# Second layer of a small MLP by seven block products in place of eight, at the end of a fused attention and MLP kernel

## The chip, the core and the metric

The kernel runs on one core of one Trainium2 chip. The metric is device microseconds of one execution: before the change the median of 3 runs is 971.51 us (971.46 to 971.6). The engines are named as in the profile: PE (TensorE matmul), PEld (its weight loads), DVE (VectorE), ACT (ScalarE), POOL (GpSimd), SP (the queue that issues nearly all DMAs).

## What is computed

Attention over 4 batches, 12 heads, 448 positions and 64 dimensions; its output is read as 1792 tokens of 768 numbers and goes through two MLPs. The change is in the last line:

```python
x = attn_out.transpose(0, 2, 1, 3).reshape(1792, 768)
h = x @ w_in;  x = (h * sigmoid(h)) @ w_out             # first MLP, 768 -> 2048 -> 768
h = x @ w_in2                                           # second MLP, 768 -> 1024
e = exp(h - max(h));  solu = h * e / sum(e)
ln = (solu - mean) / sqrt(var + 1e-6) * g_ln
out = ln @ w_out2                                       # second layer, 1024 -> 768
```

## The kernel before

All matrix products of the MLPs run in float32r with each operand split in two: a rounded half "hi" and the rest "lo". Each product is then three matmuls (list HL: hi by lo, lo by hi, hi by hi) summed in a PSUM bank.

**First MLP.** Its hidden size is cut into 8 groups g, its tokens into 4 blocks b of 512, 512, 512 and 256. A step (g, b) has two parts on PE: mlp1_a (L808, 36 matmuls) makes the hidden values, ACT applies Silu twice (L814, L815) and POOL makes the lo half (L816); mlp1_b (L831, 36 matmuls) multiplies by w_out, and DVE adds the result into x2 (L837). The list flow puts mlp1_a of a step ahead of mlp1_b of the step before.

**Weights.** They arrive as float64 bit patterns. A piece is 128x384. For each, stages() gives a chain of operations: load (L127, SP), magnitude (L135, ACT), clamp, shift, sign, low (L138 to L150, DVE), hi (L159, or L161 and L163 where the gain g_ln is folded in, ACT), lo (L171, POOL) and, for weights that are needed later, two stores to DRAM (L174). enqueue() gives every operation a due time in a clock that counts PE work (a piece every EV[0] = 3.55), and tick() issues what is due between the matmuls. During group g, ahead() queues the 8 pieces of the weights of group g+1 (fetch) and then 8 pieces of two of the ten "parked" slabs: the last group's weights, the four slabs of w_in2 and the four of w_out2. w_out2 is prepared during groups 4 and 5. A slab is 128 x 2 x 1536 (hi and lo). unpark (L725) loads it back with two DMAs of 768 KB, into the pool big as its buffers come free.

**Second MLP.** It works on 14 tiles t of 128 tokens. split (L853 POOL, L854 DVE) makes hi and lo of a tile of x2. moe2_a(t) (L922) is the first layer, 36 matmuls of 512 columns. moe2_n(t) is the softmax gate and the layer norm: peak, power, over, gate, stats, rstd, norm (L934 to L960). moe2_t (L971 to L974) turns the result with 8 transposes, and makes its halves from PSUM (hi on ACT, lo on DVE). moe2_b(t) (L995) is the second layer: two column ranges of 384, each 24 matmuls into one bank, then a copy (L1002) and a store (L1006; L1004 for the last tile, which is cut 512 and 256). In the steady state PE runs moe2_a(t), moe2_b(t-2), transposes of t-1, moe2_a(t+1) and so on.

The schedule is written out by hand (tc.manual_schedule()): each engine runs its instructions in the order in which the Python code issues them.

Of the kernel before, what the change touches and what calls it, by code (L numbers as in the profile page):

```python
# [24 lines left out]
SLAB = 1536  # L25
# [72 lines left out]
def fused_kernel(ctx: ExitStack, tc, nat, qt, gqk, w_in, w_out, w2_in, w2_out, g_ln, out):  # L98
# [9 lines left out]
    sm_ = ctx.enter_context(tc.tile_pool(name="sm", bufs=2))  # L108

    nc.scalar.preload_act_table_set("natural_log_exp_and_others")  # L110
    CL, LO = "vvvv", 'pppp'

    def stages(w, src, g, ph, c, park=None):
# [8 lines left out]
        s = slice(c * n, (c + 1) * n)  # L122
# [30 lines left out]
        def hi():  # L153
            if park is None:
                k["hi"], k["lo"] = w()[:, 0, s], w()[:, 1, s]
            else:
                k["hi"], k["lo"] = k["a"].bitcast(F32R), k["t"].bitcast(F32R)
            if g is None:
                nc.scalar.copy(out=k["hi"], in_=k["tf"])  # L159
            else:  # L160
                nc.scalar.activation(out=k["hi"], in_=k["tf"], func=AF.Identity, scale=g[:, c // 2:c // 2 + 1])  # L161
                if LO[ph] == "p":
                    nc.scalar.activation(out=k["tf"], in_=k["tf"], func=AF.Identity, scale=g[:, c // 2:c // 2 + 1])  # L163

        def lo():
            tf, h = k["tf"], k["hi"].bitcast(F32)
            if g is not None and LO[ph] == "v":
                nc.vector.scalar_tensor_tensor(out=k["lo"], in0=tf, scalar=g[:, c // 2:c // 2 + 1], in1=h,
                                               op0=ALU.mult, op1=ALU.subtract)
            else:  # L170
                en[LO[ph]].tensor_tensor(out=k["lo"], in0=tf, in1=h, op=ALU.subtract)  # L171

        def store(i):
            nc.sync.dma_start(out=park[:, i, s], in_=(k["af"], k["tf"])[i])  # L174
        return [load, mag, clamp, shift, sign, low, hi, lo] + \
            ([lambda: store(0), lambda: store(1)] if park is not None else [])

# [519 lines left out]
    STEP = ((0, 3.0, 4.2, 4.8, 5.4, 6.0, 7.2, 8.4), (0, 4.5, 5.7, 6.3, 6.9, 7.5, 8.7, 9.9, 9.9, 11.5))  # L697
# [6 lines left out]
    def enqueue(pool, keep, src, every, g=None, ph=1, at=None, park=None):  # L704
        i = len(keep)
        if park is None:
            keep.append(None)

        def w():
            if keep[i] is None:  # L710
                keep[i] = slab(pool)
            return keep[i]
        for c in range(SLAB // 384):
            if at is not None:
                last[0] = at + every * c
            else:
                last[0] = max(last[0] + every, clock[0])
            for x, f in zip(STEP[ph > 0], stages(w, src, g, ph, c, park)):
                due.append((last[0] + x, len(due), f))
        due.sort(key=lambda x: x[0])  # L720

    def unpark(pool, keep, park):
        t = slab(pool)
        for i in range(2):
            nc.sync.dma_start(out=t[:, i, :].bitcast(F32), in_=park[:, i, :])  # L725
        keep.append(t)
# [33 lines left out]
    acc1 = ctx.enter_context(tc.tile_pool(name="acc1", bufs=1, side="right", reuse_waits="tile"))  # L760
    psx = ExitStack()
    ps_mm = ctx.enter_context(tc.tile_pool(name="ps_mm", bufs=2, space=PSUM, side="right", reuse_waits="tile"))
    gp = ctx.enter_context(tc.tile_pool(name="gp", bufs=2, side="right", reuse_waits="tile"))
    cvx = ctx.enter_context(ExitStack())
    P_["cv"] = cvx.enter_context(tc.tile_pool(name="cv3", bufs=3, side="right", reuse_waits="tile"))
    x2 = [acc1.tile([128, KD, CW[0]], F32, name="x2_0")]
    big2x, psy = ExitStack(), ExitStack()

    def after_attention():
# [53 lines left out]
    def mlp1_b(i, g, b, gt):  # L823
# [15 lines left out]
        for d in range(KD):  # L839
            L.append((6 * MM[b], lambda d=d: part(d)))  # L840
        return L
# [14 lines left out]
    SPL = (0, 4, 6)  # L856
# [5 lines left out]
    for i, (g, b) in enumerate(steps):  # L862
        gt = []
        if b == 0 and 0 < g < NMG - 2:
            def ahead(g=g):
                fetch(g + 1, EV[0])
                for x in range(2 * g - 2, 2 * g):
                    enqueue(None, [], parked[x][0], EV[0], parked[x][1], ph=2 if x < 6 else 3, park=parks[x])
# [3 lines left out]
        if i == len(steps) - 1:  # L872
            def swap():
                cvx.close()
                P2["x"] = ctx.enter_context(tc.tile_pool(name="xs", bufs=3, side="right", reuse_waits="tile"))
                split(0)
            flow.append((0, swap))
        flow += mlp1_a(g, b, gt)
        if g == NMG - 1:
            def fetch2(b=b):  # L880
                for x in range(2 * b + 2, 2 * b + 4):
                    unpark(big, w2, parks[x])
# [226 lines left out]
```

## Time and profile before

| | |
|---|---|
| median of 3 runs | 971.51 us |
| the profiled execution, its own time | 971.44 us |
| its span, first to last instruction | 969.5 us |
| PE busy | 960.9 us (99%) |
| DVE, ACT, POOL busy | 69%, 46%, 43% |
| granted TensorE clock | 1.000 |
| second MLP on PE | from 718.2 us to about 966.3 us |

The table of busy shares is an average over stages with different limits; the rows of the section on the trace are taken from the stages that the change touches. An operation with a small idle time ahead of it on PE says that PE waited for nothing there.

### The profile page before, as it was taken

Reading aid. Unit: us, or ns where it says so; the run is one execution under the profiler, and the core shown is the slowest. Engines: PE = TensorE matmul, PEld = TensorE weight load, DVE = VectorE, ACT = ScalarE, POOL = GpSimd, SP = SyncE. Lnnn points to the kernel's source line nnn. Section 1 sums busy time; section 2 is a strip of 40 time slices with the busy share of each in tenths; the row PEclk is TensorE's granted clock in tenths of the full one; section 3 lists DMA queues with packets and bytes.
Section 4 is the critical chain, followed back from the end, with each engine's and each line's share of the span. In section 5 each row is a group of like instructions: output and inputs, shape, how many; then the busy total and the mean of one; then the engine's idle time right before and its main releaser. Section 6 shows DMA issues by size and latency. Waiting matters only on the chain.

```text
span 969.5 us, 15059 instructions
## 1 busy us (share of the span) xinstructions
PE 960.9 (99%) x5128; PEld 798.6 (82%) x5128; DVE 672.7 (69%) x1335; ACT 442.1 (46%) x1072; POOL 412.4 (43%) x577
## 2 busy tenths in 40 slices
PE   8999999999999999999999999999999999999998
PEld 8766667767778888888888888888888989999898
DVE  7899999999645789798888888842236535435441
ACT  6998999999722333433433453521102212212121
POOL 7888889888433434444444434431110100101000
PEclk9999999999999999999999999999999999999999
DMA  6776858775312236546364464853330000000001
GB/s 201 201 208 169 226 165 221 198 206 142 113 37 65 79 96 193 156 128 198 102 199 140 141 201 123 278 187 130 135 126 1 24 27 17 33 17 17 33 17 49
DMA packets 56717, 121.16 MB, mean 125 GB/s; under 512 B 9984, under 2 KB 32384, under 8 KB 56640
## 3 DMA queue, kind: packets, MB, share of 16 engines
q1 hardware_dynamic: 56352, 120.19, 41.3%
q8 instruction: 41, 0.67, 0.3%
q14 instruction: 36, 0.29, 0.1%
q10 hardware_dynamic: 288, 0.01, 0.0%
HBM read 77.08 MB, written 21.23 MB: 101 GB/s over the span
## 4 chain that ended last, share of the span: by engine, by line
PE 87%; DVE 5%; ACT 3%; DMA 2%; issue 1%; POOL 1%; SPq 0%; DVEq 0%; POOLq 0%; ACTq 0%
PE hp L808 24%; PE xps L831 24%; PE op L995 12%; PE h L922 12%; PE sp L445 4%; PE pv L540 4%; PE tp L497 3%; DVE sp L453 2%; ACT p L464 1%; PE lp L971 1%; PE pv L543 1%; DVE ms L281 1%; ACT ht L526 1%; DMA nat<-nat 1%; ACT qk L276 1%
## 5 line engine op out<-in xcount | busy, mean ns | idle before, releaser
L808 PE MATMUL hp<-xt,slab 128*128 128x512 f32 (+1 forms) x1152 | 238.1, 364 | 0.0
L831 PE MATMUL xps<-gt,slab 128*128 128x512 f32 (+1 forms) x1152 | 235.8, 363 | 0.0
L808 PEld LDWEIGHTS hp<-xt,slab 128*128 128x128 f32 x1152 | 197.0, 189 | 34.3 <-issue 0.7
L831 PEld LDWEIGHTS xps<-gt,slab 128*128 128x128 f32 x1152 | 197.3, 189 | 33.9
L837 DVE TENSOR_TENSOR x<-xps,x 128x512 f32<-128x512 f32 (+1 forms) x168 | 103.3, 619 | 87.1 <-PE xps L831 86.6
L816 POOL TENSOR_TENSOR gt<-gf,gt 128x512 fp32r<-128x512 f32 (+1 forms) x64 | 78.0, 1218 | 143.3 <-ACT gt L815 127.7
L995 PE MATMUL op<-slab,lt 128*128 128x384 f32 (+2 forms) x672 | 119.3, 335 | 0.0
L922 PE MATMUL h<-slab,xh 128*128 128x512 f32 x504 | 118.1, 392 | 0.0
L995 PEld LDWEIGHTS op<-slab,lt 128*128 128x128 f32 x672 | 116.2, 188 | 1.9
L453 DVE TENSOR_SCALAR_CACHE_REDUCE sp<-sp,ms 128x448 f32<-128x448 f32 x168 | 109.2, 684 | 8.1 <-PE sp L445 5.5
L922 PEld LDWEIGHTS h<-slab,xh 128*128 128x128 f32 x504 | 93.6, 188 | 19.1
L489 POOL TENSOR_SCALAR p<-p,st 128x448 f32<-128x448 f32 x144 | 97.7, 689 | 18.2 <-DVE st L480 10.4
L464 ACT ACTIVATE p<-sp,st 128x448 f32<-128x448 f32 x144 | 96.6, 687 | 6.6 <-DVE sp L453 6.2
L955 POOL TENSOR_SCALAR sm<-sm 128x1 f32<-128x1 f32 x14 | 2.7, 191 | 209.5 <-DVE sm L954 201.7
L814 ACT ACTIVATE gf<-hp 128x512 f32<-128x512 f32 (+1 forms) x64 | 34.8, 543 | 120.9 <-PE hp L808 120.2
L171 POOL TENSOR_TENSOR slab<-cvt,slab 128x384 fp32r<-128x384 f32 x48 | 51.6, 1075 | 82.9 <-ACT slab L159 82.9
L497 PE MATMUL tp<-ident,p 128*128 128x128 f32 x504 | 77.4, 274 | 1.2 <-ACT ht L526 0.9
L159 ACT CAST slab<-cvt 128x384 fp32r<-128x384 f32 x48 | 24.7, 514 | 106.4 <-DVE cvt L150 106.4
L497 PEld LDWEIGHTS tp<-ident,p 128*128 128x128 f32 x504 | 60.8, 140 | 11.2 <-ACT ht L526 2.7
L938 ACT ACTIVATE e<-h,sm 128x512 f32<-128x512 f32 x26 | 17.6, 683 | 109.7 <-DVE sm L935 109.7
L146 DVE SCALAR_TENSOR_TENSOR cvt<-raw,cva 128x384 uint32<-128x384 uint32 x88 | 63.6, 723 | 4.7 <-DVE cva L142 0.4
L171 POOL TENSOR_TENSOR cvt<-cvt,cva 128x384 fp32r<-128x384 f32 x40 | 44.0, 1102 | 52.9 <-issue 29.7
(119 smaller groups left out, 1434.0 us busy)
## 6 DMA issues: line engine op xcount, KB each, us to landing
Z<-X SPq DMA_DIRECT2D x92, 224.0 KB, 3.7
raw<-w_in SPq DMA_DIRECT2D x48, 384.0 KB, 3.4
raw<-w_out SPq DMA_DIRECT2D x48, 384.0 KB, 3.2
slab<-park SPq DMA_DIRECT2D x20, 768.0 KB, 6.2
nat<-nat SPq DMA_DIRECT2D x23, 480.0 KB, 4.0
park<-cva SPq DMA_DIRECT2D x40, 192.0 KB, 1.9
park<-cvt SPq DMA_DIRECT2D x40, 192.0 KB, 2.9
vn<-nat SPq DMA_DIRECT2D x24, 256.0 KB, 3.9
```

What stands on the lines that cost most here:

```text
L146: nc.vector.scalar_tensor_tensor(out=k["t"], in0=k["hw"], scalar=0xC0000000, in1=k["a"], op0=ALU.bitwise_and, op1=ALU.bitwise_or)
L171: en[LO[ph]].tensor_tensor(out=k["lo"], in0=tf, in1=h, op=ALU.subtract)
L453: nc.vector.tensor_scalar(out=sp, in0=sp, scalar1=c["ms"][:, g:g + 1], scalar2=None, op0=ALU.mult, op1=ALU.min, accum_out=c["st"][:, 0, i: ...
L464: nc.scalar.activation(out=P(i), in_=c["sp"][i][:, :], func=AF.Exp, bias=c["st"][:, 0, i:i + 1], scale=-1.0, accum_out=c["st"][:, 1, i:i + 1])
L489: nc.gpsimd.tensor_scalar(out=p, in0=p, scalar1=r, scalar2=0.0, op0=ALU.mult, op1=ALU.add)
L497: nc.tensor.transpose(tp[:, o + t * 128:o + (t + 1) * 128], p[:, a:a + 128], ident[:, :])
L808: nc.tensor.matmul(hp[0][:, 0:CW[b]], ws[g][0][:, pw, kd * 256 + m * 128:kd * 256 + (m + 1) * 128], xT[(b, kd)][:, px, :], start=(i == 0), ...
L816: nc.gpsimd.tensor_tensor(out=gt[0][:, 1, m, :], in0=gf[:, :], in1=gt[0][:, 0, m, :].bitcast(F32), op=ALU.subtract)
L831: nc.tensor.matmul(xps[:, 0:CW[b]], ws[g][1][:, pw, m * 768 + d * 128:m * 768 + (d + 1) * 128], gt[0][:, px, m, :], start=(j == 0), stop=( ...
L837: nc.vector.tensor_tensor(out=x2[b][:, d, :], in0=xps[:, 0:CW[b]], in1=x2[b][:, d, :], op=ALU.add)
L922: nc.tensor.matmul(h2[:, half, :], xh[:, px, kd, :], wt[:, pw, (kd % 3) * 512:(kd % 3 + 1) * 512], start=(i == 0), stop=(i == 3 * KD - 1))
L995: nc.tensor.matmul(op[:, 0:c1 - c0], lt[:, px, k, :], wt[:, pw, o + c0:o + c1], start=(i == 0), stop=(i == 23))
```

## The change

A pair of token tiles is taken as a 2x2 block matrix: A11 and A12 are the two 512-wide halves of the even tile (after the transposes), A21 and A22 those of the odd one. w_out2 with its gain is the 2x2 matrix of 512x384 blocks W11 to W22. The product is made by Strassen's scheme in Winograd's form: S1 = A21+A22, S2 = S1-A11, S3 = A11-A21, S4 = A12-S2, T1 = W12-W11, T2 = W22-T1, T3 = W22-W12, T4 = W21-T2, and seven block products A11 W11, A12 W21, S2 T2, S1 T1, S3 T3, S4 W22, A22 T4 instead of eight.

- **Weights.** enqueue4 takes the four blocks of one 384-wide column piece together: after the gain (ACT, now one operation), DVE makes T1, T3, T2 and T4; seven results are split into halves (hi on ACT, lo on POOL) in a tile "stg" of three buffers and stored with one DMA of 384 KB each. There are seven slabs of w_out2 in DRAM instead of four. The other parked weights use the same stg tile.
- **Tokens.** x2 is also stored to DRAM (x2d) and from tile 4 on loaded back by pairs (stage), so that its room is free for the second MLP; the last three of the seven slabs are loaded there.
- **Second layer.** Per pair: four copies of the transposed halves to SBUF (take), four mixes (S1, S2 on POOL; S3, S4 on DVE), seven splits (cast: ACT, DVE), seven products of 12 matmuls of 384 columns, three copies of partial sums out of PSUM (snap, ACT), three additions (add, DVE), one plain copy (ACT).
- The last pair uses another order of the products (ENDING), and what was after each product is put in by the table hooks.

```diff
+    def enqueue4(src, every, park, c, g):
+        q = {}
+        for x in ("11", "12", "22", "21"):
+            i = 2 * int(x[0]) + int(x[1]) - 3
+            push(stages(src[i], c, 2, {y: p[:, :, s] for y, p in park.items()}, None if g is None else g(x, c), (x, q)),
+                 every)
...
+        def sub(o, a, b):
+            def f():
...
+                nc.vector.tensor_tensor(out=q[o], in0=q[a], in1=q[b], op=ALU.subtract)
+            return f
+        if name == "11":
+            base += out("11", 9.3)
+        elif name == "12":
+            base += [(9.5, sub("T1", "12", "11"))] + out("T1", 10.3)
+        elif name == "22":
+            base += [(9.5, sub("T3", "22", "12"))] + out("22", 9.3) + out("T3", 10.5) + \
+                [(11.1, sub("T2", "22", "T1"))] + out("T2", 11.9)
+        else:
+            base += out("21", 9.3) + [(11.2, sub("T4", "21", "T2"))] + out("T4", 12.0)
...
+    def stage(p):
+        xs[p, "f"] = P2["f"].tile([128, KD, 256], F32, name="xf", tag="xf")
+        nc.sync.dma_start(out=xs[p, "f"][:, :, :], in_=x2d[p // 2][:, :, p % 2 * 256:p % 2 * 256 + 256])
...
+    STEPS = (("11", "11", 0), ("12", "21", 2), ("S2", "T2", 0), ("S1", "T1", 1), ("S3", "T3", 0), ("S4", "22", 1),
+             ("22", "T4", 0))
+    ENDING = (("11", "11", 0), ("12", "21", 2), ("22", "T4", 3), ("S2", "T2", 0), ("S1", "T1", 1), ("S3", "T3", 0),
+              ("S4", "22", 1))
...
+    def cast(x, f):
+        s_ = parts[x] = P2["s"].tile([128, 2, 512], F32R, name="S", tag="S")
+        nc.scalar.copy(out=s_[:, 0, :], in_=f[:, :])
+        nc.vector.tensor_tensor(out=s_[:, 1, :], in0=f[:, :], in1=s_[:, 0, :].bitcast(F32), op=ALU.subtract)
...
-        for c0, c1 in cuts:
-            op = ps_mm.tile([128, 512], F32, name="op", tag="mm")
-            i = 0
-            for k in range(8):
-                wt = w2[4 + k // 2]
-                for px, pw in HL:
-                    o = (k % 2) * 768
-                    nc.tensor.matmul(op[:, 0:c1 - c0], lt[:, px, k, :], wt[:, pw, o + c0:o + c1],
-                                     start=(i == 0), stop=(i == 23))
+        for i, (a, w, b) in enumerate(ENDING if last else STEPS):
...
+            for k in range(4):
                 for px, pw in HL:
+                    nc.tensor.matmul(op[b][:, 0:384], parts[a][:, px, k * 128:(k + 1) * 128],
+                                     W[w][:, pw, k * 384:(k + 1) * 384], start=(n[b] == 1 and j == 0),
+                                     stop=(j == 11), skip_group_check=True)
...
+            if a == "11":
+                snap("P1", 0)
...
+                cast("S4", raws["S4"])
+            elif a == "12":
+                add(0, 0, 2, "P1")
...
+            elif a == "S2":
+                snap("U2", 0)
+            elif a == "S1":
+                snap("P5", 1)
+            elif a == "S3":
+                add(1, 384, 0, "P5")
...
+            elif a == "S4":
+                add(0, 384, 1, "U2")
...
+    for p in range(1, NPR + 1):
+        a, b = 2 * p, 2 * p + 1
+        if p < NPR:
+            if p > 1:
+                turned(a - 2)
+            hs[a] = moe2_a(a)
+            early()
+            turned(b - 2)
+            n = norm(a)
+            do(n[0:3])
+            later(nc.gpsimd, n[3:8])
+            rest()
+            do(n[8:])
+            if p + 1 < NPR:
+                split(a + 2)
+            hs[b] = moe2_a(b)
+            n = norm(b)
+            if p + 1 < NPR:
+                hooks = {0: [lambda: split(b + 2)], 2: n[0:1], 3: n[1:3], 4: n[3:]}
...
+            else:
+                hooks = {0: n[0:3], 1: n[3:4], 2: n[4:6], 3: n[6:8], 4: n[8:] + [lambda: turned(a), early],
+                         6: [lambda: turned(b), lambda: cast("22", raws["22"]), lambda: later(nc.vector)]}
+            moe2_b(p - 1, hooks)
```

PE, second layer, before: one tile in the steady state (op is the PSUM tile of a column range, slab the weights, lt the halves of the turned tile).

```order
L995 MATMUL op_8545<-slab_7676,lt_8483 128x384 x6
L995 MATMUL op_8545<-slab_7679,lt_8483 128x384 x6
L995 MATMUL op_8545<-slab_7879,lt_8483 128x384 x6
L995 MATMUL op_8545<-slab_7882,lt_8483 128x384 x6
L995 MATMUL op_8581<-slab_7676,lt_8483 128x384 x6
L995 MATMUL op_8581<-slab_7679,lt_8483 128x384 x6
L995 MATMUL op_8581<-slab_7879,lt_8483 128x384 x6
L995 MATMUL op_8581<-slab_7882,lt_8483 128x384 x6
```

PE, the same place after the change: one pair of tiles (S is one of the seven split blocks).

```order
L1104 MATMUL op_8902<-slab_7753,S_8807 128x384 x12
L1104 MATMUL op_8925<-slab_7756,S_8810 128x384 x12
L1104 MATMUL op_8902<-slab_7955,S_8843 128x384 x12
L1104 MATMUL op_8958<-slab_7958,S_8846 128x384 x12
L1104 MATMUL op_8902<-slab_8205,S_8850 128x384 x12
L1104 MATMUL op_8958<-slab_8208,S_8917 128x384 x12
L1104 MATMUL op_8902<-slab_8211,S_8939 128x384 x12
```

A tile had 48 matmuls, a pair 96; a pair now has 84, in seven runs of 12, and the bank op_8902 is filled, copied out and added to four times.

DVE, preparation of w_out2 during group 4, after the change (cva and cvt are the working tiles of a piece, xps the PSUM tile of the first MLP; L157 to L169 are the former L138 to L150, L889 the former L837, L189 is new).

```order
L157 TENSOR_SCALAR cva_6546<-cva_6546 128x384
L189 TENSOR_TENSOR cvt_6471<-cvt_6507,cvt_6471 128x384
L889 TENSOR_TENSOR x2_3_3922<-xps_6571,x2_3_3922 128x256
L161 TENSOR_SCALAR cva_6546<-cva_6546 128x384
L889 TENSOR_TENSOR x2_3_3922<-xps_6581,x2_3_3922 128x256
L165 SCALAR_TENSOR_TENSOR cvt_6547<-raw_6492,cva_6546 128x384
L169 SCALAR_TENSOR_TENSOR cvt_6547<-raw_6492,cvt_6547 128x384
L189 TENSOR_TENSOR cvt_6518<-cvt_6507,cvt_6518 128x384
```

Before, the same stretch held L138, L142, L146, L150 and L837 alone; the subtractions L189 (four for each four pieces) stand between them, behind the gain on ACT that they read.

DVE, one pair in the steady state, after the change (S splits, raw and mixed are the blocks in SBUF, h2 the first layer's result of the odd tile).

```order
L1050 TENSOR_TENSOR S_9383<-mixed_9375,S_9383 128x512
L1050 TENSOR_TENSOR S_9386<-mixed_9373,S_9386 128x512
L1058 TENSOR_TENSOR raw_9358<-raw_9301,raw_9358 128x512
L1050 TENSOR_TENSOR S_9390<-raw_9358,S_9390 128x512
L1058 TENSOR_TENSOR raw_9308<-raw_9308,mixed_9375 128x512
L1014 BN_AGGR sm_9368<-sm_9368 128x2
L1020 TENSOR_SCALAR e_9367<-e_9367,sm_9368 128x1024
L916 TENSOR_TENSOR xh_9398<-xf_9193,xh_9398 128x768
L1050 TENSOR_TENSOR S_9457<-raw_9308,S_9457 128x512
L916 TENSOR_TENSOR xh_9460<-xf_9193,xh_9460 128x768
L1089 TENSOR_TENSOR ob_9440<-op_9463,sn_9455 128x384
L1050 TENSOR_TENSOR S_9477<-raw_9365,S_9477 128x512
```

The splits of S2, S1, S3, S4 and A22 stand around the end of the even tile's norm; before, this place held the norm and two splits for each tile.

## Rows read from the trace of the kernel before

**Rows 1.** The page, parts 1 and 2: busy us and shares; tenths in 40 slices.
```profile
PE 960.9 (99%) x5128; PEld 798.6 (82%) x5128; DVE 672.7 (69%) x1335; ACT 442.1 (46%) x1072; POOL 412.4 (43%) x577
PE   8999999999999999999999999999999999999998
```

**Rows 2.** Waits of PE, whole program: who, for whom, us, times, longest.
```profile
PE tp L245 <- POOL ident masks.py:199: 1.3, 1, 1.3
```

**Rows 3.** Timeline of PE over one tile: start, us, operation, count.
```profile
852.45 8.51 PE L995 MATMUL op<-slab,lt 128*128 128x384 f32 x48
860.79 1.03 PE L971 MATMUL lp<-ident,e 128*128 128x128 f32 x8
861.59 8.45 PE L922 MATMUL h<-slab,xh 128*128 128x512 f32 x36
869.87 8.51 PE L995 MATMUL op<-slab,lt 128*128 128x384 f32 x48
```

**Rows 4.** Groups by form, 780 to 930 us: busy us, mean ns | idle before.
```profile
L947 DVE SCALAR_TENSOR_TENSOR e<-h,sm,e 128x512 f32<-128x512 f32 x18 | 12.7, 746 | 0.3
L938 ACT ACTIVATE e<-h,sm 128x512 f32<-128x512 f32 x18 | 12.2, 683 | 81.5 <-DVE sm L935 81.5
L951 DVE BATCH_NORM_STATS2 sm<-e 128x6 f32<-128x512 f32 x18 | 11.5, 680 | 0.0
L934 DVE TENSOR_REDUCE sm<-h 128x2 f32<-128x1024 f32 x9 | 11.0, 1225 | 52.4 <-PE h L922 52.4
L974 DVE TENSOR_TENSOR lt<-lp,lt 128x512 fp32r<-128x512 f32 x16 | 10.3, 686 | 6.5 <-ACT lt L973 6.5
L973 ACT CAST lt<-lp 128x512 fp32r<-128x512 f32 x16 | 8.6, 589 | 0.1
```

**Rows 5.** First preparation of w_out2, 545 to 578 us: busy by engine, then groups.
```profile
545.00:578.00 33.00, 33.00 (x164) 28.03 (x164) 27.04 (x49) 17.51 (x33) 14.72 (x13) 1.00 0.59 186
L171 POOL TENSOR_TENSOR cvt<-cvt,cva 128x384 fp32r<-128x384 f32 x8 | 9.3, 1160 | 13.5 <-ACT cvt L163 7.2 <-issue 6.4
L150 DVE SCALAR_TENSOR_TENSOR cvt<-raw,cvt 128x384 uint32<-128x384 uint32 x9 | 7.5, 839 | 0.3
L816 POOL TENSOR_TENSOR gt<-gf,gt 128x512 fp32r<-128x512 f32 x4 | 5.2, 1296 | 4.7 <-ACT gt L815 3.4 <-DMA raw<-w_out 1.3
L837 DVE TENSOR_TENSOR x<-xps,x 128x256 f32<-128x256 f32 x6 | 2.5, 420 | 0.6 <-PE xps L831 0.5
```

**Rows 6.** Timeline of POOL: first and last of 8 pieces, then two slab pieces.
```profile
549.13 1.34 POOL L171 TENSOR_TENSOR cvt<-cvt,cva 128x384 fp32r<-128x384 f32 x1 [3.17 <-ACT cvt L163]
...
577.33 1.29 POOL L171 TENSOR_TENSOR cvt<-cvt,cva 128x384 fp32r<-128x384 f32 x1 [3.31 <-issue]
...
591.74 1.02 POOL L171 TENSOR_TENSOR slab<-cvt,slab 128x384 fp32r<-128x384 f32 x1 [2.50 <-ACT slab L159]
...
605.96 1.01 POOL L171 TENSOR_TENSOR slab<-cvt,slab 128x384 fp32r<-128x384 f32 x1 [2.36 <-ACT slab L159]
```

**Rows 7.** Timeline of PE and DVE around the start of group 6.
```profile
602.93 8.32 PE L808 MATMUL hp<-xt,slab 128*128 128x512 f32 x36
...
604.18 0.56 DVE L146 SCALAR_TENSOR_TENSOR cvt<-raw,cva 128x384 uint32<-128x384 uint32 x1
...
606.09 1.30 DVE L146 SCALAR_TENSOR_TENSOR cvt<-raw,cva 128x384 uint32<-128x384 uint32 x1
```

**Rows 8.** The stretch of four slab loads: busy by engine, clock, DMA, GB/s.
```profile
690.00:695.00 5.00, 5.00 (x24) 4.14 (x23) 2.57 (x4) 0.21 (x1) 1.29 (x1) 1.00 1.02 423
```

**Rows 9.** The end, and DMA issues (count, KB each, us to landing).
```profile
966.55 0.37 ACT L1002 COPY ob<-op 128x256 f32<-128x256 f32 x1 [2.24 <-PE op L995]
...
raw<-w_out SPq DMA_DIRECT2D x48, 384.0 KB, 3.2
park<-cva SPq DMA_DIRECT2D x40, 192.0 KB, 1.9
y<-ob SPq DMA_DIRECT2D x1, 128.0 KB, 1.7
```

More of the change, by code (lines that the diff above doesn't have):

```diff
@@ L165, in lo @@
[L165 to L174, printed above, removed]
@@ L175, in stages, with gain @@
-        return [load, mag, clamp, shift, sign, low, hi, lo] + \
-            ([lambda: store(0), lambda: store(1)] if park is not None else [])
+        base = list(zip(STEP[ph], (load, mag, clamp, shift, sign, low)))
+        if quad is None:
+            return base + list(zip(STEP[ph][6:], halves(lambda: k["tf"], w, CL[ph])))
+        name, q = quad
+        def gain():
+            if g is not None:
+                nc.scalar.activation(out=k["tf"], in_=k["tf"], func=AF.Identity, scale=g)
+            q[name] = k["tf"]
@@ L702, in tick, with push, enqueue @@
             due.pop(0)[2]()
-    def enqueue(pool, keep, src, every, g=None, ph=1, at=None, park=None):
+    def push(fs, every, at=None):
+        last[0] = at if at is not None else max(last[0] + every, clock[0])
+        for x, f in fs:
+            due.append((last[0] + x, len(due), f))
+        due.sort(key=lambda x: x[0])
+    def enqueue(pool, keep, src, every, ph=1, at=None, park=None):
         i = len(keep)
@@ L872, in fused_kernel @@
         if i == len(steps) - 1:
[L873 to L877, printed above, removed]
+            flow += [(0, lambda: split(0)), (0, lambda: split(1))]
         flow += mlp1_a(g, b, gt)
@@ L1028, in fused_kernel @@
         tick(dur)
[L1029 to L1032 removed]
+    assert not due
     psx.close()
     P2["l"] = ctx.enter_context(tc.tile_pool(name="ps_l", bufs=2, space=PSUM, side="right", reuse_waits="tile"))
[L1035 to L1059 removed]
@@ new lines, in fused_kernel @@
+    split(2)
+    hs[1] = moe2_a(1)
+    n = norm(1, ())
+    do(n[0:1])
+    split(3)
+    tp = [turn(0, half) for half in range(2)]
+    mlp1.close()
+    P2["e"] = ctx.enter_context(tc.tile_pool(name="me", bufs=3, reuse_waits="tile"))
+    P2["1"] = ctx.enter_context(tc.tile_pool(name="m1", bufs=6, reuse_waits="tile"))
+    P2["s"] = ctx.enter_context(tc.tile_pool(name="ms", bufs=5, reuse_waits="tile"))
+    P2["w"] = ctx.enter_context(tc.tile_pool(name="mw", bufs=3, reuse_waits="tile"))
+    P2["f"] = ctx.enter_context(tc.tile_pool(name="mf", bufs=1, reuse_waits="tile"))
@@ new lines, in fused_kernel @@
+    P2["x"] = ctx.enter_context(tc.tile_pool(name="mx", bufs=2, reuse_waits="tile"))
+    P2["2"] = ctx.enter_context(tc.tile_pool(name="m2", bufs=2, reuse_waits="tile"))
+    P2["3"] = ctx.enter_context(tc.tile_pool(name="m3", bufs=4, reuse_waits="tile"))
+    lns[1] = P2["e"].tile([128, 2, 512], F32, name="e", tag="e")
+    do(n[1:3])
+    for x in USED[4:]:
+        W[x] = unpark(P2["w"], None, park2[x])
+    stage(2)
+    for half in range(2):
+        take(0, half, tp[half])
+    do(n[3:])
```

285 lines of the change are left out of this document (165 added, 120 removed).

## The prediction, made before the changed kernel ran

> **What bounds the kernel now.** I read the page first: PE is busy 99% of the span, and every slice from the second on shows nine tenths or more [rows 1]. A busy PE need not be a working one, so the list of who waited for whom came next: the longest wait of PE in the whole program is 1.3 us, at the very start [rows 2]. So the time is the sum of PE's instructions, and a change is worth what it takes out of that sum, as long as nothing else becomes late. Then the timeline of PE in the second MLP [rows 3]: over one tile the starts of the operations follow one another without a hole. From start to start moe2_b takes 860.79 - 852.45 = 8.34 us (48 matmuls of 384 columns, 0.1738 us each), the 8 transposes 861.59 - 860.79 = 0.80, moe2_a 869.87 - 861.59 = 8.28. The printed durations are some tenths longer, because ends are modelled; I take start to start. The groups by form [rows 4] show DVE and ACT with long idle times ahead of the operations that wait for PE (52.4 us ahead of 9 peaks): they follow PE here. In the stage where w_out2 is prepared it is different: DVE is busy 27.04 of 33 us, POOL 14.72 [rows 5].
>
> **The matmuls.** 14 tiles of 48 are 672; 7 pairs of 7 x 12 are 588. The other matmuls and the transposes stay. 84 x 0.1738 = 14.60 us go, all of it from the chain that sets the end. Form, width and weight loads of the 588 are those of before, so their price is a row of the same thing. Each run of 12 starts behind two waits, but waits that are already met have no visible price: moe2_a and moe2_b follow one another without a hole [rows 3].
>
> **What comes in beside PE, steady state.** A pair has 32.8 us on PE (2 x 8.28 + 1.6 + 84 x 0.1738). DVE gets per pair three more splits (0.69 each), two mixes and three additions of 384 columns (below 0.69 each): some 5 us on top of 16; ACT some 5 on top of 7; POOL two sums of 128x512, 1.30 each by the nearest row of that size [rows 4, 5]. No engine is near 32.8. What can hurt is latency, since all queues are in order. I count from the end of moe2_a of the even tile, t = 0. Transposes until 0.8, two copies on ACT (0.59) until 2.0, S1 and S2 on POOL until 4.6, S2's hi until 5.2. On DVE peak, then (after ACT's two powers, 0.68 each) over, two gates of 0.75 and two stats of 0.68 stand ahead of S2's lo: about 6.9, so lo is there at 7.6. PE wants S2 after 0.8 + 8.28 (moe2_a of the odd tile) + 2 products of 2.085 = 13.25. That is 5.6 us of cover. S3 is ready near 10.5 and wanted at 17.4; S4 stands behind norm and a split, ready near 15, wanted at 19.5. The copies of partial sums have a product of 2.085 us between the end of one fill of a bank and the start of the next, against 0.6 for the copy. So these edits cost nothing; if the cover were gone, each us of lateness would cost 6 us, once per pair before the last.
>
> **Where the cover is thin.** With the last odd tile, peak and both powers move ahead of the copy U2 in ACT's queue, because its norm is spread over the products. My count has that copy end 0.2 us after PE wants the bank. In the last pair all splits follow one another with no moe2_a beside them; S3 there misses its time by about 0.2. The transposes of tile 1, whose norm has only one moe2_a beside it, by 0.1. Together 0.5; nothing in the trace shows these places, so I bound them with 0 and 2 us, and take 0.5 because the count is made of rows of the same operations.
>
> **The end.** Before, a copy of 256 columns (0.37) and a store of 128 KB (1.7) follow the last matmul; then it is an addition of 384 columns on DVE, between 0.42 for 256 [rows 5] and 0.69 for 512 [rows 4], say 0.55, and a store of 192 KB, 1.9 as for a store of that size to DRAM [rows 9]: +0.4 (0 to 0.8).
>
> **The weights, earlier.** Per four pieces there are four subtractions on DVE and seven outputs instead of four. In the 33 us of the first preparation that is 8 x 0.56 (an unhindered DVE operation of the same size [rows 7]) = 4.5 us more on DVE, and 6 x 1.16 = 7.0 more on POOL [rows 5]. DVE then has 31.5 of 33 at least. DVE and POOL hinder one another: with POOL in a slab operation from 605.96 to 606.97, DVE's next one takes 1.30 us, and 0.56 without [rows 6, 7]. With subtractions at the hindered mean of 0.84 and all new POOL time on top, DVE would need 27.0 + 6.7 + 7.0 = 40.7: 7.7 us late at the end of the stage. Who needs it? The next slab is w_in of group 6: its last piece is done at 591.74 + 1.02 = 592.8, and PE starts on it at 602.93 [rows 6, 7]: 10.2 us of cover. A hidden-layer bank of the first MLP is filled in half a section (4.1 us) and wanted again two sections (16.3) after its start: 12.2 us for ACT. So 0 to 7.7 us late costs PE nothing. The second preparation (groups 5 and 6) feeds slabs that are loaded long after.
>
> The outputs go through three buffers. Eight pieces take (577.33 - 549.13) / 7 = 4.03 us each [rows 6], so seven outputs have 16.1 us, 2.3 each, and a buffer may be held 6.9 us. I count hi 0.6, lo 1.2, store 3.2 (a load of 384 KB; two stores of 192 KB would be 3.8) [rows 4, 5, 9]: 5.0 to 5.6, and queueing. It fits, not by much.
>
> **Loads at the turn.** Three slabs and the first token pair, 5.5 MB, are loaded only when the first MLP's room is free. Four loads together moved 423 GB/s [rows 8], so 13 us. Between the end of the first MLP on PE and the fifth product of the first pair lie three moe2_a, two sets of transposes and four products: 34.8 us. The stores of x2 and SP's order stand ahead of it, but twice the time would still fit.
>
> **Sum.** 971.44 (the profiled execution: span 969.5 and 1.94 around it) - 14.60 + 0.5 + 0.4 = 957.7. The median of the runs is 0.07 above that execution, so 957.8.
>
> **Rivals.**
> - *Late weights.* To the 7.7 us of lateness come waits of DVE for the gain on ACT that each subtraction reads, up to 0.6 each by the nearest ACT row [rows 4], 8 x 0.6 = 5. Then w_in of group 6 is 12.7 - 10.2 = 2.5 us late: 960.3. For it: DVE's share and the hindrance. Against: not every wait comes on top. [...] Chance 0.13.
> - *Seven starts are not free.* If every run of 12 begins with a hole of 0.1 us, 49 x 0.1 = 4.9: 962.7. Against: no hole at any border of rows 3. It takes in the case that splits come late by about 0.8 us beyond their cover in each pair. Chance 0.06.
> - *Slower: the three output buffers hold up ACT.* ACT waits for a free stg buffer, and behind it in its queue stand Silu and the magnitudes of the next pieces. If a buffer is held h us, a preparation of 14 outputs is late by 14 x (h/3 - 2.3). At h = 12 that is 23.8 us; the first costs 23.8 - 10.2 = 13.6, the second (cover 12.2, ACT's) 11.6: 983. It turns slower from h of about 10.8, where the two cost 14. For it: SP is one queue in order, and a store that waits for POOL keeps the next load behind it. Against: my count of h is half of that. Chance 0.04.
> - *Nothing gained.* The seven products could go at a lower rate than the eight, for instance by weight loads: 971. But the form is the same. Chance 0.02.
>
> **How the numbers follow.** Forecast 0.75, with its own range of 956.8 (all small terms 0) to 959.5 (2.0 and 0.8, rounded). 8 in 10 needs a part of the late weights too: 956.7 to 961.0. A change of 0.2% (1.9 us) is about what a measurement of this kernel tells from none: faster 0.93, the same 0.02 (nothing gained), slower 0.05 (the buffers, and mechanisms that I don't see).
>
> **What would show it.** Right: PE with 588 matmuls of 384 columns in the second layer at 0.174 us from start to start; a pair of 32.8 us; no wait of PE above 0.5 us after the first MLP; two preparations with DVE above 90%. Wrong: waits of PE on DVE or ACT ahead of a product in each pair (then the latency count fails), a hole ahead of mlp1_a of group 6 or of a Silu bank (then the preparation), or on a slab load at the fifth product (then the turn).

## The result, and the profile after

The changed kernel takes **958.91 us** (median of 4 runs, 958.33 to 959.2) against 971.56 us of the kernel before in the same session (971.46 to 971.84): ratio 0.9869, 95% interval 0.9852 to 0.9886. The forecast was 957.8 with a range of 956.7 to 961.0. So it is 1.1 us slower than forecast, and the range holds it.

The profiled execution took 958.81 us, its span is 957.0. In the kernel after, some lines have other numbers: mlp1_a is L860, mlp1_b L883, Silu L866 and L867, its lo half L868, moe2_a L982, the transposes L1035, the block products L1104, the copies of partial sums (snap) L1086, the additions L1089; in the preparation shift to low are L161 to L169, the gain L179, the subtractions L189, hi L124, lo L127, the store of stg L130 and the load of a slab L768.

The page of the kernel after, part 1 (busy us, share of the span), against [rows 1]:

```profile
PE 946.0 (99%) x5044; PEld 784.5 (82%) x5044; DVE 715.1 (75%) x1410; ACT 471.6 (49%) x1133; POOL 443.5 (46%) x601
```

PE has 84 matmuls less and 14.9 us less of busy time; DVE, ACT and POOL have 42, 30 and 31 us more and are still far from the span. The timeline of PE over one pair of tiles, against [rows 3]:

```profile
774.18 8.44 PE L982 MATMUL h<-slab,xh 128*128 128x512 f32 x36
...
791.51 14.75 PE L1104 MATMUL op<-slab,S 128*128 128x384 f32 x84
806.10 1.04 PE L1035 MATMUL lp<-ident,e 128*128 128x128 f32 x8
806.89 8.44 PE L982 MATMUL h<-slab,xh 128*128 128x512 f32 x36
```

From start to start a pair takes 806.89 - 774.18 = 32.71 us (32.8 were counted), and seven products 806.10 - 791.51 = 14.59, which is 0.1737 per matmul. Two tiles took 2 x 17.42 = 34.84 us before [rows 3], so a pair gives 2.13 us. No row of PE in this stretch has an idle time, and no row of the last two pairs has one either:

```profile
922.33 10.59 PE L1104 MATMUL op<-slab,S 128*128 128x384 f32 x60
...
933.55 4.44 PE L1104 MATMUL op<-slab,S 128*128 128x384 f32 x24
...
938.62 14.81 PE L1104 MATMUL op<-slab,S 128*128 128x384 f32 x84
```

The list of PE's waits (who, for whom, us, times, longest) has one of 1.0 us behind the attention that the kernel before lacks:

```profile
PE hp L860 <- ACT gt L867: 1.0, 1, 1.0
```

The timeline of PE shows its place:

```profile
640.49 8.32 PE L883 MATMUL xps<-gt,slab 128*128 128x512 f32 x36
649.77 8.45 PE L860 MATMUL hp<-xt,slab 128*128 128x512 f32 x36 [0.96 <-ACT gt L867]
658.07 2.20 PE L883 MATMUL xps<-gt,slab 128*128 128x512 f32 x9
```

The same place in the kernel before (mlp1_b is L831 there, mlp1_a L808) has no wait:

```profile
639.91 8.32 PE L831 MATMUL xps<-gt,slab 128*128 128x512 f32 x36
648.07 8.32 PE L808 MATMUL hp<-xt,slab 128*128 128x512 f32 x36
```

After the change, mlp1_b should be followed at 640.49 + 8.16 = 648.65; mlp1_a starts at 649.77 and takes 8.30 us to the next start where its neighbours take 8.16. That is 1.26 us in all. It falls at the end of the second preparation of w_out2.

**Where the span's 12.5 us came from**, from the starts on PE in both traces: the second MLP, from the second moe2_a to PE's end, takes 220.72 us where it took 235.63: -14.91. The wait above: +1.26. The first MLP starts at 254.82 where it started at 254.23: +0.58. From PE's end to the end of the span it is 3.78 where it was 3.21: +0.57. PE's end is its last start plus the prices from start to start, because the printed ends are modelled. The sum is -12.50. The rows, two of before and then three of after, the last of them the final addition on DVE, which stands where [rows 9] have a copy at 966.55:

```profile
254.23 4.34 PE L808 MATMUL hp<-xt,slab 128*128 128x512 f32 x18
730.66 8.35 PE L922 MATMUL h<-slab,xh 128*128 128x512 f32 x36
254.82 4.34 PE L860 MATMUL hp<-xt,slab 128*128 128x512 f32 x18
732.50 8.35 PE L982 MATMUL h<-slab,xh 128*128 128x512 f32 x36
953.47 0.56 DVE L1089 TENSOR_TENSOR ob<-op,sn 128x384 f32<-128x384 f32 x1 [1.00 <-PE op L1104]
```

The chain of work that ended last, just ahead of PE's late start (start, us, what):

```profile
644.40 1.03 POOL stg L127
...
645.46 0.57 DVE cvt L165
...
646.61 0.48 DVE cvt L189
...
647.16 0.07 ACT stg L124
...
647.58 0.62 ACT cvt L179
...
648.64 0.59 ACT gf L866
649.24 0.49 ACT gt L867
```

This is the preparation of the last weight piece, going from POOL to DVE and on to ACT, with a Silu behind it in ACT's queue. DVE had waited 1.89 us for POOL ahead of 645.46: by the code L165 writes a working tile (cvt, three buffers) that POOL's lo half had still to read. In the link that ended last the wait is thus for a working tile, not for an output buffer. Silu reads a PSUM bank that PE had filled some 12 us earlier, at half of the section that ends at 640.49, and PE waits for that bank.

### The profile page after: what moved, and what is told of

Read it like the earlier page. It is cut to its first block, busy times and chain, and to the rows that moved or that the text cites. A ratio compares the mean times of both kernels' runs of the same rounds, so it can differ in the third digit from the quotient of the medians.

```text
span 957.0 us, 15017 instructions
## 1 busy us (share of the span) xinstructions
PE 946.0 (99%) x5044; PEld 784.5 (82%) x5044; DVE 715.1 (75%) x1410; ACT 471.6 (49%) x1133; POOL 443.5 (46%) x601
## 5 line engine op out<-in xcount | busy, mean ns | idle before, releaser
L860 PE MATMUL hp<-xt,slab 128*128 128x512 f32 (+1 forms) x1152 | 238.2, 364 | 1.0 <-ACT gt L867 1.0
L883 PE MATMUL xps<-gt,slab 128*128 128x512 f32 (+1 forms) x1152 | 235.7, 363 | 0.0
L860 PEld LDWEIGHTS hp<-xt,slab 128*128 128x128 f32 x1152 | 197.0, 189 | 35.5 <-ACT gt L867 1.4
L883 PEld LDWEIGHTS xps<-gt,slab 128*128 128x128 f32 x1152 | 197.3, 189 | 33.8
L889 DVE TENSOR_TENSOR x<-xps,x 128x512 f32<-128x512 f32 (+1 forms) x168 | 102.4, 618 | 68.6 <-PE xps L883 68.3
L868 POOL TENSOR_TENSOR gt<-gf,gt 128x512 fp32r<-128x512 f32 (+1 forms) x64 | 78.7, 1230 | 126.4 <-ACT gt L867 111.7
L982 PE MATMUL h<-slab,xh 128*128 128x512 f32 x504 | 117.8, 392 | 0.0
L982 PEld LDWEIGHTS h<-slab,xh 128*128 128x128 f32 x504 | 93.6, 188 | 18.8
L1104 PE MATMUL op<-slab,S 128*128 128x384 f32 x588 | 103.6, 335 | 0.0
L1104 PEld LDWEIGHTS op<-slab,S 128*128 128x128 f32 x588 | 102.2, 188 | 0.5
L127 POOL TENSOR_TENSOR slab<-cvt,slab 128x384 fp32r<-128x384 f32 x48 | 51.8, 1079 | 82.7 <-ACT slab L124 82.7
L866 ACT ACTIVATE gf<-hp 128x512 f32<-128x512 f32 (+1 forms) x64 | 34.7, 542 | 106.5 <-PE hp L860 105.4
L127 POOL TENSOR_TENSOR stg<-cvt,stg 128x384 fp32r<-128x384 f32 x52 | 56.8, 1100 | 56.8 <-ACT stg L124 55.7
L124 ACT CAST slab<-cvt 128x384 fp32r<-128x384 f32 x48 | 24.6, 514 | 107.6 <-DVE cvt L169 107.6
L165 DVE SCALAR_TENSOR_TENSOR cvt<-raw,cva 128x384 uint32<-128x384 uint32 x88 | 63.6, 723 | 10.4 <-POOL stg L127 4.9
L473 PE MATMUL sp<-Z 128*128 128x448 f32 x138 | 64.2, 466 | 2.2 <-ACT X L417 1.1
L473 PE MATMUL sp<-X,lz 128*128 128x448 f32 x168 | 63.3, 379 | 0.5 <-POOL lz L413 0.5
```

Source lines behind the costliest of these rows:

```text
L127: en[e].tensor_tensor(out=k["o"][1], in0=f(), in1=k["o"][0].bitcast(F32), op=ALU.subtract)
L473: nc.tensor.matmul(sp[:, :], a_, k_, start=(w == 0), stop=(w == len(mm) - 1))
L860: nc.tensor.matmul(hp[0][:, 0:CW[b]], ws[g][0][:, pw, kd * 256 + m * 128:kd * 256 + (m + 1) * 128], xT[(b, kd)][:, px, :], start=(i == 0), ...
L868: nc.gpsimd.tensor_tensor(out=gt[0][:, 1, m, :], in0=gf[:, :], in1=gt[0][:, 0, m, :].bitcast(F32), op=ALU.subtract)
L883: nc.tensor.matmul(xps[:, 0:CW[b]], ws[g][1][:, pw, m * 768 + d * 128:m * 768 + (d + 1) * 128], gt[0][:, px, m, :], start=(j == 0), stop=( ...
L889: nc.vector.tensor_tensor(out=x2[b][:, d, :], in0=xps[:, 0:CW[b]], in1=x2[b][:, d, :], op=ALU.add)
```

## Experiments

Two questions: is the price of a product what it was taken for, and where do the covers end; and what makes the second preparation late. The line numbers below are those of the kernel after (one more behind L1058 where S1 is repeated).

### What a product costs: one product twice

```diff
-    STEPS = (..., ("S4", "22", 1), ("22", "T4", 0))
+    STEPS = (..., ("S4", "22", 1), ("22", "T4", 0), ("22", "T4", 0))
```

and ("S4", "22", 1) twice in ENDING; what follows a product in the code stands behind the second of the two.

> The last product of each pair is done twice (12 more matmuls of 384 columns per pair, 84 in all; the sums it goes into are therefore not the reference's). Theory 'PE is the bound and a product costs its matmuls': 958.9 + 84 x 0.1738 = 973.5. Theory 'part of the gain of 14.6 us was given back to waits in the second MLP that an extra product would cover': less than 973.5, by the size of these waits. Theory 'each run of 12 has a price of its own': more than 973.5, 0.7 us for every 0.1 us of price.

Measured: 975.88 us (975.42 to 977.12), 17.0 more than the change. The timeline of PE over a pair, and at the last two pairs:

```profile
776.25 8.44 PE L982 MATMUL h<-slab,xh 128*128 128x512 f32 x36
...
811.03 8.44 PE L982 MATMUL h<-slab,xh 128*128 128x512 f32 x36
...
950.62 0.44 PE L1104 MATMUL op<-slab,S 128*128 128x384 f32 x1 [1.38 <-ACT S L1049]
```

A pair takes 34.78 us, 2.07 more than 32.71, for 12 matmuls: 0.173 each, so seven pairs cost 14.5. The rest is an accident of this edit: in the last pair but one the hooks make the last pair's A22 ahead of the added product, which reads that one and waits for it (2.2 us from start to start, in two waits). In the profiles that is all: 14.5 + 2.2 = 16.7, as the spans differ (973.7 and 957.0). The first MLP starts 0.4 us later here, but the wait ahead of its mlp1_a is 0.48 us instead of 0.96, and the second MLP starts where it did (732.48 and 732.50). So the price is linear, and the seven products give back nothing to waits that an eighth would hide.

### How much cover the mixes have: S1 repeated on POOL

```diff
-        e.tensor_tensor(out=raws[o][:, :], in0=raws[a][:, :], in1=raws[b][:, :],
-                        op=ALU.add if x == "S1" else ALU.subtract)
+        for _ in range(N + 1 if x == "S1" and e is nc.gpsimd else 1):
+            e.tensor_tensor(out=raws[o][:, :], in0=raws[a][:, :], in1=raws[b][:, :],
+                            op=ALU.add if x == "S1" else ALU.subtract)
```

with N = 3, then 6, then 4.

> POOL's sum S1 is computed 4 times instead of once in each pair before the last (3 x 1.33 us more on POOL, the same result). The count of the prediction gives S2 5.6 us and S4 4.5 us of cover, so 4.0 us fit: no wait of PE on a product, 958.9. If the latency of the mixes were on the path of PE, each pair would cost up to 4 us: 980.

Measured: 961.53 us, 2.6 more than expected. A pair takes 32.74 us, so 4.0 us more on POOL cost the pairs nothing. But the place in the last pair but one that the prediction called thin gives way (timeline of PE):

```profile
922.94 8.51 PE L1105 MATMUL op<-slab,S 128*128 128x384 f32 x48
933.23 2.38 PE L1105 MATMUL op<-slab,S 128*128 128x384 f32 x12 [1.78 <-ACT sn L1087]
```

The fifth product wants its bank at 922.94 + 4 x 2.085 = 931.28 and starts at 933.23, behind a copy of a partial sum on ACT (the copy U2): 1.95 us. Another 0.4 is a later start of the first MLP.

> The same with S1 7 times (6 x 1.33 = 8.0 us more). By the count of the prediction S2 is 2.4 us late and S4 up to 3.5 us in each of 6 pairs: 14 to 21 us more. By the trace of the changed kernel (S2 done 6.4 us and S4 5.0 us ahead of PE, and DVE free for S2 1.1 us after S2's rounded half) about 1.9 us a pair: 11 us more, 970. If PE is not held up by the mixes at all, 958.9.

Measured: 988.82 us, much more than either count. The timeline of PE over a pair:

```profile
796.25 4.35 PE L1105 MATMUL op<-slab,S 128*128 128x384 f32 x24
803.51 12.25 PE L1105 MATMUL op<-slab,S 128*128 128x384 f32 x60 [2.91 <-ACT sn L1087]
815.59 1.04 PE L1035 MATMUL lp<-ident,e 128*128 128x128 f32 x8
```

A stretch behind the wait (length, PE's busy us, granted clock, DMA share, GB/s):

```profile
804.50:807.80 3.30, 3.30 (x13) 0.54 0.03 7
```

Two things come together. The third product starts at 803.51 instead of 796.25 + 24 x 0.1738 = 800.42: it waits not for S2's lo (DVE has it at 763.7 in the first pair, where the third product starts at 766.03), but for ACT's copy of P1, which must read the bank before the product adds to it, and stands in ACT's queue behind the rounded halves of S2, S1 and S3. And behind this stop of 3.1 us, from 1 us after it on (1.00 until 804.50), the granted clock is 0.54 for about 3.3 us, so that 60 matmuls take 815.59 - 803.51 = 12.08 us instead of 10.43. That makes 4.74 us a pair: 28.4 in six pairs, and 1.1 for U2's place.

> S1 on POOL 5 times (4 x 1.33 = 5.3 us more). Theory 'the copy of P1 stands in ACT's queue behind the rounded halves of S2, S1 and S3': with 8.0 us more PE stood 3.1 us, so its cover is 4.9 us and PE waits 0.4 us per pair, 2.4 us in 6 pairs; with the last pair's place (1.9 us at 4.0, 3.3 at 5.3) 958.9 + 2.4 + 3.3 = 964.6. Theory of the prediction, 'S2 itself is what PE waits for' (cover 5.6): no wait in the pairs, 962.2.

Measured: 970.25 us (967.77 to 971.65, an unusually wide spread), 5.7 more than the nearer of the two counts. A pair takes 34.06 us, 1.35 more, in two waits (timeline of PE):

```profile
762.88 8.59 PE L1105 MATMUL op<-slab,S 128*128 128x384 f32 x48 [0.19 <-ACT sn L1087]
772.09 2.38 PE L1105 MATMUL op<-slab,S 128*128 128x384 f32 x12 [0.61 <-DVE ob L1090]
```

The copy of P1 is late by 762.88 - 762.51 = 0.37 us, as expected (0.4). The larger part was in no theory: the seventh product (the last 12) wants the bank that an addition on DVE has to read first, and this addition stands in DVE's queue behind S4's lo and a split. With U2's copy the wait is now 2.67 us, and the 12 matmuls behind it take 3.5 us for 2.1, at a granted clock of 0.59. The spread goes with the clock: of the ten runs the three with a mean granted clock of 1.000 took 967.77 to 968.55 us, the seven with 0.998 took 969.71 to 971.65.

### P1's copy moved forward in ACT's queue

moe2_a of the odd tile and the first product are issued before rest(), so that ACT's order is S2, P1, S1, S3; the orders of the other engines stay. N = 6.

```diff
-            rest()
-            do(n[8:])
-            if p + 1 < NPR:
-                split(a + 2)
             hs[b] = moe2_a(b)
...
             if a == "11":
                 snap("P1", 0)
-                if last:
-                    rest()
+                mid()
```

> S1 on POOL 7 times as before, but the copy of P1 is put into ACT's queue ahead of the rounded halves of S1 and S3 (the orders of PE, DVE and POOL stay). Theory 'P1's copy behind the mixes in ACT's queue holds PE': the stop of PE before the third product falls from 3.1 to 0.8 us a pair, the stretch at half clock behind it goes, S4 is then up to 2 us late: 958.9 + 6 x 2.8 + 2 = 978, at most 982 and at least 966. Theory 'S2 is late': P1's copy changes nothing, 988.8.

Measured: 989.18 us: a miss, the time is as without the edit. The mechanism is there (timeline of PE, a pair and then a row of the last pair but one):

```profile
795.96 4.35 PE L1105 MATMUL op<-slab,S 128*128 128x384 f32 x24
800.65 4.61 PE L1105 MATMUL op<-slab,S 128*128 128x384 f32 x24 [0.34 <-ACT sn L1087]
806.09 2.55 PE L1105 MATMUL op<-slab,S 128*128 128x384 f32 x13 [0.82 <-ACT sn L1087]
808.96 2.19 PE L1105 MATMUL op<-slab,S 128*128 128x384 f32 x11 [0.33 <-DVE S L1050]
812.73 2.38 PE L1105 MATMUL op<-slab,S 128*128 128x384 f32 x12 [1.59 <-DVE ob L1090]
...
959.06 3.99 PE L1105 MATMUL op<-slab,S 128*128 128x384 f32 x12 [5.39 <-ACT sn L1087]
```

The stop ahead of the third product falls from 3.1 to 0.5 us, and the clock stays at 1.00 through the pair. But three more waits take its place, at the fifth, sixth and seventh product, and a pair takes 37.11 us where it took 37.46. What the pairs save is lost in the last pair but one, where PE now stops 5.39 us for U2's copy and the next 12 matmuls take 3.82 us for 2.09, at a granted clock of 0.54. The expectation had looked at S4 and not at what stands behind it. So the cover of the whole chain is what counts: 4.0 us late cost nothing, 5.3 cost 1.35, 8.0 cost 4.4 (here, at a granted clock of 1.00 and with P1's copy moved). By these it is 3.6 to 4.0 us. At 5.3 us the largest part of a pair's loss is the wait for the bank of the seventh product, and at 8.0 with P1's copy moved it is the largest wait of the pair too.

### What makes the second preparation late

The kernel after, timeline of ACT: the hi halves that go into stg, and Silu behind one of them:

```profile
619.11 0.52 ACT L124 CAST stg<-cvt 128x384 fp32r<-128x384 f32 x1 [1.49 <-DVE cvt L189]
...
627.65 0.51 ACT L124 CAST stg<-cvt 128x384 fp32r<-128x384 f32 x1 [3.91 <-DMA parkT<-stg]
628.07 0.59 ACT L866 ACTIVATE gf<-hp 128x512 f32<-128x512 f32 x1
```

The DMAs of SP beside them:

```profile
617.75 0.97 SPq L768 DMA_DIRECT2D slab<-park  x2
621.05 0.52 SPq L130 DMA_DIRECT2D parkT<-stg  x1
```

DVE's row for T4:

```profile
631.53 1.35 DVE L189 TENSOR_TENSOR cvt<-cvt 128x384 f32<-128x384 f32 x1 [3.17 <-POOL stg L127]
```

T1's buffer is taken at 619.11, its store is issued at 621.05 behind a slab load of 1.5 MB, and it is free at 627.6: 8.5 us, of which the store took 6.5 from issue to landing, against a median of 2.7. ACT stands for 3.91 us, and with it Silu and POOL's lo halves; DVE waits 3.17 us for POOL with T4. Three candidates were tried: the ring of three output buffers, the slab load, the work on DVE. A fourth, the ring of three working tiles (cvt) that DVE waits for, was not, and no run gave either ring a fourth buffer.

A measure for all of them: in the five other runs that leave this preparation as it is (eighth, and S1 repeated), PE's wait ahead of the same mlp1_a is printed as 0.48, 0.98, 1.02, 1.04 and 1.24 us. So only a wait that falls out of 0.48 to 1.24 us tells something.

**Two buffers for three** (bufs=2 for stg).

> Two stg buffers in place of three. Theory 'the ring of output buffers holds up ACT': with a hold of 5.0 to 5.6 us per buffer, 14 outputs come late by 14 x (5.3/2 - 2.3) = 4.9 us more; the second preparation has no cover left, so PE waits some 5 us more there: about 964. The first preparation has cover of 10 us and adds little. Theory 'work of DVE and POOL, not the buffers': two buffers do as well as three, 958.9 to 959.5.

Measured: 966.39 us (965.04 to 966.66), 7.5 more. Waits of ACT in this stage (who, for whom, us, times, longest):

```profile
ACT stg L124 <- DMA parkT<-stg: 14.9, 4, 5.0
```

Waits of PE:

```profile
PE hp L860 <- ACT gt L867: 6.3, 3, 3.0
```

With two buffers the ring is on the path; with three this does not tell how much of the wait is the ring's. The waits are 5.3 us more than the 0.96 of the change, as expected. Of the excess over the expected 5 us, 1.7 us is the clock again (timeline of PE, and a stretch behind its second row):

```profile
640.32 4.38 PE L860 MATMUL hp<-xt,slab 128*128 128x512 f32 x18 [2.79 <-ACT gt L867]
655.88 10.05 PE L860 MATMUL hp<-xt,slab 128*128 128x512 f32 x36 [3.02 <-ACT gt L867]
```

```profile
655.88:659.50 3.62, 3.62 (x9) 0.53 0.34 126
```

Behind the last wait (3.02 us) mlp1_a takes 10.05 us for 8.32, with a granted clock of 0.53 over 3.6 us. Behind the wait of 2.79 us before it the clock stayed at 1.00.

**The slab load later.**

```diff
-        if g == NMG - 2 and b < 2:
-            flow.append((0, lambda b=b: unpark(P_["big2"], ws[NMG - 1], parks[b])))
+        if (g, b) in ((6, 0), (7, 0)):
+            flow.append((0, lambda b=g - 6: unpark(P_["big2"], ws[NMG - 1], parks[b])))
```

> Only the load of the last group's w_out slab (1.5 MB, two DMAs) is issued one section later, at the start of step (7,0) instead of (6,1). Theory 'load ahead of the stores': in the changed kernel this load was issued at 617.75, the store of a stg buffer at 621.05, and ACT waited for that buffer until 627.65; with the load gone from there the 3.9 us wait of ACT on parkT falls below 1 us, Silu is on time and the 0.96 us wait of PE goes: 957.6. Theory 'too much work for DVE and POOL': ACT still ends the preparation late, PE still waits about 1 us: 958.9. The load may instead meet the stores of 637 to 645; then the wait is as long or longer there, 959 to 960.

Measured: 958.51 us (958.18 to 958.85). PE waits 0.63 us instead of 0.96, which is within what the runs without this edit show. The store of T1 now lands in 2.8 us, and ACT takes the buffer 1.1 us earlier, at 626.51. But the load, now issued at 638.16, meets a later store: ACT waits once for 4.0 us there. So the load does lengthen a hold, but this edit only moved the place; it doesn't tell what the wait would be without it.

**Less work on DVE.**

```diff
-        base = list(zip(STEP[ph], (load, mag, clamp, shift, sign, low)))
+        base = list(zip(STEP[ph], (load, mag, (lambda: None) if quad else clamp, shift, sign, low)))
```

> The clamp of w_out2's pieces is left out (the weights need none), 8 operations of 0.35 to 0.95 us less on DVE in each of the two preparations. Theory 'DVE's work is too much in the second preparation': its end comes 3 to 5 us earlier, the 0.96 us wait of PE goes: 957.6. Theory 'the output buffers and the order of DVE and POOL around them': DVE only waits longer for POOL and for buffers, the wait of PE stays at 0.5 to 1 us: 958.4 to 958.9.

Measured: 957.24 us (956.97 to 958.18). The last hi half of the preparation starts at 646.34 instead of 649.61, the Silu in question at 645.37 instead of 648.64, and PE doesn't wait (0.5 us of both differences is an earlier start of the first MLP; with a start as early, 254.25, the run with S1 five times waited 1.04 us). ACT still waits 3.8 us for a store. So DVE's operations are on the chain too, though DVE isn't full: it is busy 12.51 of 18 us, then 14.26 of 18 (stretches of the kernel after: length, busy us of PE, PEld, DVE, ACT, POOL):

```profile
614.00:632.00 18.00, 18.00 (x89) 15.25 (x89) 12.51 (x27) 9.20 (x18) 8.76 (x8) 1.00 0.79 280
632.00:650.00 18.00, 17.04 (x76) 13.81 (x75) 14.26 (x25) 8.88 (x18) 8.41 (x9) 1.00 0.48 175
```

So DVE's operations are part of the cause; whether the buffers alone would do as well was not tried. The preparation is one chain over four in-order queues, DVE to ACT to POOL to SP and back through the buffers, and ending it 2.7 us earlier frees PE.

**More time.**

```diff
-                        enqueue4(w2_out, EV[0], park2, x - 6, gln4)
+                        enqueue4(w2_out, 5.5 if g == NMG - 3 else EV[0], park2, x - 6, gln4)
```

> Only the pieces of w_out2's second preparation (column pieces 2 and 3) are due every 5.5 instead of every 3.55, so that it stretches into group 6, where nothing else is prepared. If the lateness of this preparation is what made PE wait before mlp1_b at 649.77 (0.96 us, 1.26 us with what follows it), the wait disappears and the time is 1.3 us below that of the changed kernel: about 957.6. If the wait has nothing to do with the preparation, it stays, at 958.9. If slower pieces hold buffers longer and only move the wait to a later Silu, a wait of about 1 us shows up between 655 and 680.

Measured: **957.64 us** (957.12 to 957.88), ratio to before 0.9853 (0.9839 to 0.9866). The wait is gone and none has come in its place (timeline of PE):

```profile
640.90 8.32 PE L883 MATMUL xps<-gt,slab 128*128 128x512 f32 x36
649.06 8.32 PE L860 MATMUL hp<-xt,slab 128*128 128x512 f32 x36
657.22 3.11 PE L883 MATMUL xps<-gt,slab 128*128 128x512 f32 x13
```

The intervals of the two ratios overlap, but the runs don't (957.12 to 957.88 here, 958.33 to 959.2 for the change), and the row without the wait shows where the 1.3 us came from: the first MLP starts at 255.23 here, as in two runs that waited 0.48 and 1.02 us. It is the version to keep: the same work, later.

### The start of the first MLP

> The kernel before once more, for its profile alone. In its first profile the first MLP began on PE at 254.23 us; in five profiles of the changed kernel and its variants at 254.73 to 255.23, with a wait of 1.1 to 1.5 us near 23 us in the attention that the profile of before lacks. If this is how the start of an execution happens to fall, the second profile of before shows such a start too; if it comes from the change, it shows 254.2 again.

Measured: the second profile of before starts the first MLP at 254.25, as in the first. Ten profiles of the change and its variants lie between 254.25 and 255.23 (three of them at 254.25, 254.28 and 254.54), so the change does not always bring the later start; their orders of instructions in the first 25 us, as far as the timelines show, are the same as before. So the 0.58 lies in a spread that reaches from before's value upwards. In the late ones PE waits 1.1 to 1.5 us near 23 us; the DMAs of Z beside it took up to 6.3 us from issue to landing, and up to 4.6 in the two profiles of before. Whether the change widens that spread stays open.

## Why the prediction was right, and where it failed

- *The matmuls, -14.60.* Right. The second MLP gave 14.91, 0.31 more than counted: 7 pairs at 2.13 us where 12 matmuls make 2.09, the rest lying in shorter distances between the other rows. The added products cost 0.173 us per matmul. "Seven starts are not free" and "Nothing gained" are out: 32.71 us a pair, no hole.
- *Steady state costs nothing; smallest cover S4's 4.5 us, S2's 5.6.* Right in the result: no wait. In size the count was somewhat high: measured 3.6 to 4.0 us. Wrong in the place. The prediction counted when each split is ready; what is late first are the operations that free a PSUM bank, P1's copy on ACT and an addition on DVE, because they stand behind the mixes in the same queues. An operand comes late only behind them (S4's lo, 0.33 us, with 8.0 us more and P1's copy moved). And "each us of lateness would cost 6 us" leaves out what can come behind a stop: one of 3.1 us cost a pair 4.7, with the granted clock at 0.54 behind it.
- *Thin places, +0.5.* Measured 0: U2's copy ended some 0.6 us in time where the count had it 0.2 late. But the place was the right one: with 4.0 us more on POOL it is the one that costs 1.95 us.
- *The end, +0.4.* Measured 0.57, within its bounds.
- *The weights, "0 to 7.7 us late costs PE nothing".* **This is the step that failed**: +1.26. It gave the second preparation no consumer ("feeds slabs that are loaded long after"). Its slabs are indeed late for nobody. But its instructions stand in ACT's queue ahead of Silu, and PE waits for Silu. The cover for that was given as 12.2 us, and the chain came later than that. The prediction's own sign for this failure, a hole ahead of a Silu bank, is what the trace shows; and the two runs that ended the preparation earlier or stretched it (the clamp left out, pieces every 5.5) took the hole away. The first preparation did stay covered: no wait of PE there.
- *DVE above 90% in both preparations.* Half right: 29.32 and then 31.70 of 33 us busy from 545 on, in and behind the first, but 70% and 79% in the second, where DVE waits for POOL and for buffers. The count of busy time on one engine was the wrong measure there.
- *Rival "Slower: the three output buffers hold up ACT".* Its mechanism took place: ACT stood 3.91 us once for an output buffer. How much of PE's 1.26 us is owed to that no run separates; the rival had 25 us. The hold of 5.0 to 5.6 us was about right for a store that flies alone (4.8 us for T1 where the slab load was moved: taken at 619.03, landed at 623.8), and it was 8.5 us where a slab load is ahead of it: over the 6.9 allowed, and below the 10.8 from which it would have turned the sign. The prediction had weighed slab loads at the turn only.
- *Late weights* (w_in of group 6) did not happen, and the loads at the turn made no wait. The upper count of 7.7 us, with all new POOL time on top of DVE's own, was an estimate; measured is that DVE was busy 61.02 us from 545 to 611 where it had been 56.00.

Term by term: second MLP -14.91 (forecast -14.10 with the thin places), end +0.57 (+0.4), preparation +1.26 (0), start +0.58 (0): -12.50 of the span where -13.7 was forecast. Three terms came out 2.0 us worse than forecast and one 0.8 better, so that the forecast missed by 1.1 to 1.2 only is in part luck; the range would have held the 2.0 as well.

## What to carry to other kernels

Work that is taken away from the engine that sets the time is worth its rows, start to start (here 14.91 us for 14.60 counted); look for the price in what the change adds to the in-order queues of the others. For each added operation ask not only who needs its result, but what stands behind it in its queue: here a Silu and a copy that free a bank were late before any operand was. Where a background stage runs late and has free time behind it, spread it out before you look for buffers or engines to relieve it: here that took 958.91 us to 957.64.

## What the runs showed of the hardware

- A stop of TensorE can cost more than its length. Behind stops of about 3.0 us (2.92 with S1 seven times, 3.02 with two stg buffers) the granted clock was 0.53 to 0.54 over 3.3 to 3.6 us, and the matmuls there took 1.65 to 1.73 us longer. In stretches of 1 us it read 1.00, 0.62, 0.50, 0.50, 0.67 and 1.00 behind the stop of 2.92 us (first pair, from 766.0 on), and 0.54, 0.50, 0.50, 0.75 and 1.00 behind the one of 3.02 (from 656.0 on). The length of a stop alone does not tell whether it falls: behind one of 2.67 us (S1 five times) it was 0.59 over 3.5 us, behind one of 2.79 us (two stg buffers) it stayed at 1.00. With four stops of 0.5 to 1.9 us a pair, 4.3 us in all (P1's copy moved), it stayed at 1.00 too; in the same run it was 0.54 behind a stop of 5.4 us. The prediction had priced waits at their length alone.
- A 384 KB store landed in 2.7 us (the median of 16) and in 6.5 behind a 1.5 MB load that had been issued 3.3 us earlier on the same queue; with that load moved away the same store landed in 2.8.
